# One stream of FFN blocks in written order: the scheduler is switched off for the main loop of a DFT + GeGLU kernel

## The chip, the cores and the metric

The kernel runs on one core of a Trainium2 chip. The metric is the device time of one execution in microseconds (us). Five engines work side by side, each on its own queue of instructions: TensorE (PE, with its weight loads shown as PEld), VectorE (DVE), ScalarE (ACT), GpSimd (POOL) and SyncE (SP). Transfers are issued from SP's queue, a few from ACT's, and the loads that change the type from POOL's.

## The reference

The input `x` has 8 batches of 3008 tokens with 256 channels. A two-dimensional Fourier transform over tokens and channels is taken of each batch and its real part kept; then every token goes through a gated feed-forward block (FFN) with 1536 hidden columns.

```
X = fft(fft(x, axis=1), axis=2).real          # x: (8, 3008, 256)
t = X.reshape(24064, 256)
out = (gelu(t @ w_gate) * (t @ w_val)) @ w_out # 256 -> 1536 -> 256
```

## The kernel before

**Half of the tokens carry all.** The transform of real input is symmetric, so for each batch only `HALF` = 1505 token columns are computed, split by symmetry into an even part E and an odd part O (`EO_sb`). E + O gives a token's value and E - O that of the mirrored token. The 1505 columns form three chunks of 512, 512 and 481.

**The transform of a batch** (`dft_work`) is a list of 37 entries, each a closure that issues a few instructions. Eight are `s1_pack`: eight small matmuls each of `x_sb` with `G` (`s1_mm`, L372) into two `ps_dft` banks, one copy by ACT to `up_sb` (L397) and two adds by DVE into `A_sb` (L400); each is followed by an empty entry. Twelve are `ch_pack` (four matmuls, L420, and a copy to `Z_sb`, L427). The remaining nine are `e_pack`, `b_pack` and `o_pack` for each chunk (L442, L470, L488), which write `EO_sb`, and `EB_sb` by a small trip through DRAM. Batch 0 is transformed in a head, which is written inside `tc.manual_schedule()`; the transform of batch b+1 is the *filler* in the FFN of batch b.

**The FFN of a batch** is 3 chunks x 12 hidden blocks = 36 blocks, called slots here. A block has five big matmuls (L541). Two, WgE and WgO, make the gate in `ps_g`, which ACT turns into `gelu_sb` (L557). WgM is then added to the same bank, which turns it into the mirrored gate, and ACT reads it again (L566). WvE makes the even value in `ps_v`; DVE reads it and adds channel 128, `ve_sb` (L575). WvO is added to the same bank; DVE multiplies gelu and value into `h_sb` (L586), makes the mirrored value `v_sb` (L588), and POOL multiplies that with the mirrored gelu into the second half of `h_sb` (L590). The second layer of a chunk is 24 pieces of four matmuls (L615) into `ps_o`; they run two per slot in the slots of the next chunk; each sixth piece is followed by a copy to `out_sb` on ACT (L635) and four stores on SP (L531).

**The order in which a slot is written** is that of the string `SLOT`:

```
SLOT = "GgVLvLf"   # G: gate, block fc   g: mirrored gate, block fc-1
                   # V: even value, fc   v: rest of the value, fc-1
                   # L: a second-layer piece   f: filler
```

Each chunk has a loop of 13 turns: the thirteenth does only `g` and `v` of the chunk's last block, and the next chunk starts with a turn that has no `g` and no `v`. The filler entries are spread evenly: entry count times (slot + 1) over 36.

**The input of the next transform.** `load_x` (L156) is one transfer for each half of a batch, issued on POOL's queue, which turns f32 into bf16 on the way, into one of two `x_sb` buffers. The call stands at the top of the batch loop: for b > 0, batch b+1 is loaded by the turn b of the loop, and `filler = dft_work(b + 1)` of the same turn reads it. The loads of batch 1 stand at the end of the head.

**What sets the order.** Inside `tc.manual_schedule()` each engine's queue has the instructions in the order in which the program writes them. Outside of it, as in the main loop before, Tile's scheduler puts them in order: it walks the same list with its own costs, and an instruction whose inputs are there may stand ahead of one that was written before it, on every engine, POOL's loads among them.

Of the kernel before, what the change touches and what calls it, by code (L numbers as in the profile page):

```python
# [18 lines left out]
def _sub(base: bass.AP, free_pattern, free_offset, part_start=0, part_num=None):  # L19
    p_step, p_count = base.ap[0]  # L20
    if part_num is None:
        part_num = p_count - part_start
    pat = [[p_step, part_num]] + [list(x) for x in free_pattern]
    off = base.offset + part_start * p_step + free_offset
    return ap_replace(base, ap=pat, offset=off)
# [11 lines left out]
def kernel(  # L37
# [10 lines left out]
    B, T, C = x.shape  # L48
# [6 lines left out]
    NFC = F // 128  # L55
# [3 lines left out]
    groups = [list(range(1, 9)), list(range(9, 17)), list(range(17, 24)) + [0]]  # L59
# [26 lines left out]
    G = const_pool.tile([NP, NJ, K2H * 4], BF16)  # L86
# [8 lines left out]
    def x_tile():  # L95
        return work_pool.tile([NP, NJ, C], BF16, tag="x", bufs=2, name="x_sb")
# [48 lines left out]
    x_tiles = []  # L145

    def x_src(b, p0, np_, j0, nj):
        return ap_replace(
            x,
            ap=[[NJ * C, np_], [1, nj * C]],  # L150
            offset=x.offset + (b * T + p0 * NJ + j0) * C,
        )

    def load_x(b, pieces):
        for j0, nj in pieces:
            nc.gpsimd.dma_start(out=_sub(x_tiles[b], [[1, nj * C]], j0 * C), in_=x_src(b, 0, NP, j0, nj))  # L156
# [176 lines left out]
    def fold_w(nm, q):  # L333
        def run():
            f0, n = WSL[q]
            fs = slice(f0, f0 + n)
            ps = ps_g() if nm == "g" else ps_v()
            nc.tensor.matmul(ps[:, :n], exch, w_hi[nm][:, fs], start=True, stop=True)  # L338
            lo = w_lo[nm][:, fs]
            nc.vector.scalar_tensor_tensor(W[nm, "E"][:, fs], ps[:, :n], keep, lo, op0=ALU.mult, op1=ALU.add)  # L340
            nc.vector.scalar_tensor_tensor(  # L341
                W[nm, "O"][:, fs], lo, keep, ps[:, :n], op0=ALU.mult, op1=ALU.subtract)
            if nm == "g":
                nc.scalar.activation(W[nm, "M"][:, fs], W[nm, "O"][:, fs], AF.Copy, scale=keep2)
        return run
# [308 lines left out]
    SLOT = "GgVLvLf"  # L654
# [52 lines left out]
    folds = {0: 1, 3: 2, 7: 3}  # L707
    folds = {slot: [fold_w(nm, q) for nm in ("g", "v")] for slot, q in folds.items()}
    early = head[NHEAD:]
    pend = []  # L710
    for b in range(B):
        if b + 1 < B:
            if b > 0:
                x_tiles.append(x_tile())
                load_x(b + 1, [(0, 16), (16, 16)])
            filler = dft_work(b + 1)
        else:
            filler = []
        chunks = ffn_work(b)
        nslot = len(chunks) * NFC  # L720
        first_slot = 0
        if b == 0:

            first_slot = NFC
        slot = 0
        fi = 0
        for parts, l2s in chunks:
            done = 0
            for fc in range(NFC + 1):
                for step in SLOT:  # L730
                    if step in "GV" and fc < NFC:
                        parts[step][fc]()
                    elif step in "gv" and fc > 0:
                        parts[step][fc - 1]()
                    elif step == "L" and done < len(pend) and fc < NFC:
                        pend[done]()
                        done += 1
                    elif step == "f" and fc < NFC:
                        if b == 0 and slot < NFC:
                            for _ in range(2):  # L740
                                if early:
                                    early.pop(0)()
                            for f in folds.get(slot, []):
                                f()
                        tgt = max(0, len(filler) * (slot + 1 - first_slot) // (nslot - first_slot))
                        while fi < tgt:
                            filler[fi]()
                            fi += 1
                slot += fc < NFC
            assert done == len(pend)  # L750
            pend = l2s
    for u in pend:
        u()

# [1 line left out]
_INS = ['x', 'moe_w_gate', 'moe_w_val', 'moe_w_out']  # L756
# [26 lines left out]
```

## Time and profile before

| | |
|---|---|
| three runs | 683.09 us median (682.94 to 683.29) |
| the profiled execution | 683.09 us, its span 681.3 us |
| PE busy | 643.4 us, 94% of the span |
| DVE busy | 631.2 us, 93% |
| ACT busy | 468.0 us, 69% |
| POOL busy | 356.0 us, 52% |
| first even value of batch 0 to that of batch 1 | 33.26 to 122.28 us |
| the same for batches 1 to 6 | 78.4 to 78.9 us each |
| batch 7, to its last `v_sb` | 593.81 to 664.15 us |
| `x_sb` loads, issue to landing | 6.6 to 16.0 us, median 9.1 us (14 loads) |

The span runs from the first to the last instruction; the 1.8 us between it and the profiled execution's own time lie outside the program's instructions. Busy is the time in which an engine had at least one instruction under way. Matmuls overlap in their pipeline, so that a PE that waits between two matmuls for less than the length of one still looks busy; the distance from one matmul's start to the next one's tells more. An instruction is named by engine, line and the tile that it writes: "PE ps_g L541" is a gate matmul.

### The profile page before, as it was taken

How to read it: one execution, taken by the hardware profiler on the slowest of the kernel's cores; microseconds unless marked ns; L12 is line 12 of the kernel's file. 1: busy time of each engine (PE TensorE's matmuls, PEld its weight loads, DVE VectorE, ACT ScalarE, POOL GpSimd, SP SyncE). 2: the span in 40 equal slices, each digit the busy share in tenths (PEclk: the TensorE clock that was granted, in tenths of full speed). 3: DMA queues.
4: the chain of work that ended last, by engine and by line, in shares of the span. 5: the costliest groups of instructions: out<-in, count | busy, mean ns of one | idle time of the engine just before them, and what ended most of it. 6: DMA issues, size and time to landing. Idle time of an engine off the chain costs nothing.

```text
span 681.3 us, 14441 instructions
## 1 busy us (share of the span) xinstructions
PE 643.4 (94%) x5038; PEld 432.2 (63%) x5092; DVE 631.2 (93%) x1067; ACT 468.0 (69%) x897; POOL 356.0 (52%) x345
## 2 busy tenths in 40 slices
PE   2787999999999999999999999999999999999995
PEld 1543656666666666676666666676666666666664
DVE  8699998999999999999899999999999999999990
ACT  4575668767777677776776777776777677766660
POOL 8334455456555555446554555445554545555650
PEclk9999999999999999999999999999999999999999
DMA  9780252216222342216212162221221112221123
GB/s 239 180 181 0 47 111 59 48 37 130 48 56 50 65 102 52 55 43 124 52 44 56 34 132 48 55 48 37 47 55 40 44 41 47 55 51 40 44 48 70
DMA packets 39684, 46.21 MB, mean 68 GB/s; under 512 B 7361, under 2 KB 36694, under 8 KB 38102
## 3 DMA queue, kind: packets, MB, share of 16 engines
q1 hardware_dynamic: 35834, 33.21, 20.3%
q0 software_dynamic: 3184, 11.57, 9.3%
q8 instruction: 40, 0.66, 0.4%
q10 hardware_dynamic: 592, 0.49, 0.3%
q14 instruction: 34, 0.28, 0.1%
HBM read 32.15 MB, written 24.66 MB: 83 GB/s over the span
## 4 chain that ended last, share of the span: by engine, by line
PE 82%; ACT 6%; DVE 4%; DMA 3%; issue 1%; SPq 0%; POOL 0%; ACTq 0%; DVEq 0%; POOLq 0%
PE ps_o L615 35%; PE ps_g L541 24%; PE ps_v L541 16%; DMA out_dram<-out_sb 3%; PE ps_dft L420 3%; PE ps_dft L372 2%; ACT gelu_sb L566 2%; DVE x_sb L243 2%; ACT gelu_sb L557 1%; ACT out_sb L635 1%; PE ps_dft L488 1%; PE ps_dft L442 1%; ACT Z_sb L427 1%; PE ps_g L338 1%; ACT EO_sb L492 1%
## 5 line engine op out<-in xcount | busy, mean ns | idle before, releaser
L590 POOL TENSOR_TENSOR h_sb<-gelu_sb,v_sb 128x512 bf16<-128x512 bf16 (+1 forms) x288 | 329.8, 1145 | 289.3 <-DVE v_sb L588 200.7
L615 PE MATMUL ps_o<-Wo_sb,h_sb 128*128 128x256 bf16 (+1 forms) x2232 | 341.8, 272 | 3.0 <-ACT gelu_sb L566 1.1
L615 PEld LDWEIGHTS <-h_sb 128*128 128x128 bf16 (+1 forms) x2304 | 228.6, 100 | 108.8 <-issue 3.3
L557 ACT ACTIVATE gelu_sb<-ps_g 128x512 bf16<-128x512 f32 (+1 forms) x288 | 169.6, 592 | 77.4 <-PE ps_g L541 59.7
L575 DVE SCALAR_TENSOR_TENSOR ve_sb<-EB_sb,w,ps_v 128x512 f32<-128x512 bf16 (+1 forms) x288 | 209.8, 731 | 9.4 <-PE ps_v L541 8.8
L586 DVE TENSOR_TENSOR h_sb<-gelu_sb,ps_v 128x512 bf16<-128x512 bf16 (+1 forms) x288 | 194.0, 674 | 12.0 <-ACT gelu_sb L557 5.2
L588 DVE SCALAR_TENSOR_TENSOR v_sb<-ve_sb,ps_v 128x512 f32<-128x512 f32 (+1 forms) x288 | 192.5, 668 | 0.0
L566 ACT ACTIVATE gelu_sb<-ps_g 128x512 bf16<-128x512 f32 (+1 forms) x288 | 169.5, 592 | 16.1 <-PE ps_g L541 15.7
L541 PE MATMUL ps_g<-EO_sb,WgE 128*128 128x512 bf16 (+1 forms) x285 | 107.0, 375 | 3.2 <-ACT gelu_sb L566 2.1
L541 PE MATMUL ps_v<-EO_sb,WvO 128*128 128x512 bf16 (+1 forms) x288 | 108.2, 376 | 0.6
L541 PE MATMUL ps_g<-EO_sb,WgM 128*128 128x512 bf16 (+1 forms) x282 | 104.7, 376 | 2.5 <-ACT gelu_sb L557 1.6
L541 PE MATMUL ps_v<-EO_sb,WvE 128*128 128x512 bf16 (+1 forms) x279 | 104.8, 376 | 0.1
L541 PE MATMUL ps_g<-EO_sb,WgO 128*128 128x512 bf16 (+1 forms) x252 | 94.7, 376 | 1.4 <-DVE WgO L341 1.3
L635 ACT ACTIVATE out_sb<-ps_o 128x512 f32<-128x512 f32 x92 | 55.0, 597 | 34.4 <-PE ps_o L615 28.5
L427 ACT ACTIVATE Z_sb<-ps_dft 128x512 bf16<-128x512 f32 x88 | 52.4, 599 | 16.2 <-PE ps_dft L420 15.9
L400 DVE TENSOR_TENSOR A_sb<-ps_dft,up_sb 128x384 bf16<-128x384 f32 x112 | 56.8, 548 | 4.8 <-ACT up_sb L397 4.8
L372 PEld LDWEIGHTS <-x_sb 94*128 94x128 bf16 x512 | 33.0, 101 | 29.1 <-DVE x_sb L243 19.1
L541 PEld LDWEIGHTS <-WvE 128*128 128x128 bf16 x288 | 28.1, 98 | 25.4 <-issue 3.3
L541 PEld LDWEIGHTS <-WgM 128*128 128x128 bf16 x288 | 28.1, 97 | 24.3
L397 ACT ACTIVATE up_sb<-ps_dft 128x384 f32<-128x384 f32 x56 | 27.5, 490 | 21.3 <-PE ps_dft L372 21.3
L420 PE MATMUL ps_dft<-CS,A_sb 128*128 128x128 bf16 x372 | 40.5, 222 | 1.2 <-ACT Z_sb L427 0.6
L372 PE MATMUL ps_dft<-G,x_sb 94*128 94x96 bf16 x468 | 35.6, 208 | 4.7 <-DVE x_sb L243 4.6
(104 smaller groups left out, 314.2 us busy)
## 6 DMA issues: line engine op xcount, KB each, us to landing
out_dram<-out_sb SPq DMA_DIRECT2D x361, 64.0 KB
x_sb<-in_x_dram POOLq DMA_DIRECT2D x14, 752.0 KB, 9.1
EB_sb<-row SPq DMA_DIRECT2D x14, 128.0 KB
x_plain<-in_x_dram SPq DMA_DIRECT2D x4, 384.0 KB
x_plain<-in_x_dram SPq DMA_DIRECT2D x2, 768.0 KB
EB_sb<-row SPq DMA_DIRECT2D x7, 120.2 KB
Wo_sb<-in_moe_w_out_dram POOLq DMA_DIRECT2D x2, 384.0 KB, 5.8
wg_hi<-in_moe_w_gate_dram SPq DMA_DIRECT2D x2, 256.0 KB
```

The lines of the kernel that those rows point to most:

```text
L372: nc.tensor.matmul(ps[:, jj * 96 : (jj + 1) * 96], xt[:, j0 + jj, cc * 128 : (cc + 1) * 128], G[:, j0 + jj, :], start=True, stop=True,)
L420: nc.tensor.matmul(ps[:, o : o + 128], A[:, g, k2 + d, :], CS[:, g, :], start=True, stop=True)
L427: nc.scalar.activation(dst, src, AF.Copy)
L541: nc.tensor.matmul(ps[:, :n], W[nm, part][:, fs], src, start=start, stop=stop, **kw)
L557: nc.scalar.activation(gl[:, 0, :n], pg[:, :n], AF.Gelu)
L566: nc.scalar.activation(_sub(gl, [[-1, n]], TOK + n - 1), pg[:, :n], AF.Gelu)
L575: nc.vector.scalar_tensor_tensor(ve[:, :n], EB_bufs[b][:, c0 : c0 + n], w128[:, fc : fc + 1], pv[:, :n], op0=ALU.mult, op1=ALU.add)
L586: nc.vector.tensor_tensor(st["h"][:, fc, 0, :n], gl[:, 0, :n], pv[:, :n], op=ALU.mult)
L588: nc.vector.scalar_tensor_tensor(_sub(vv, [[-1, n]], n - 1), ve[:, :n], 2.0, pv[:, :n], op0=ALU.mult, op1=ALU.subtract)
L590: nc.gpsimd.tensor_tensor(st["h"][:, fc, 1, :n], gl[:, 1, :n], vv[:, :n], op=ALU.mult)
L615: nc.tensor.matmul(pso[:m, sign, :], st["h"][:, fc, sign, h0 : h0 + m], Wo_sb[:, fc, :], start=(fc == 0), stop=(fc == NFC - 1),)
L635: nc.scalar.activation(osb[:m], pso[:m], AF.Copy)
```

## The change

The three nested loops become one function `feed` that is called inside `tc.manual_schedule()`. It lists all 288 blocks of all batches and walks them in one stream. A slot keeps its parts in the same order, gate, mirrored gate of the block before, even value, piece, rest of the value of the block before, piece, filler; the block before may now belong to the chunk or the batch before, so the turn with only `g` and `v` is left out except after the last block of all. The calls of `load_x` and `dft_work` are made at slot 0 of each batch, ahead of the slot's other parts. The pieces of the second layer, the early entries of batch 0, the weight folds and the spread of the filler are as before. The functions that issue the instructions are not changed, and neither are the pools.

```diff
@@ -707,50 +707,60 @@
     folds = {0: 1, 3: 2, 7: 3}
     folds = {slot: [fold_w(nm, q) for nm in ("g", "v")] for slot, q in folds.items()}
     early = head[NHEAD:]
-    pend = []
-    for b in range(B):
-        if b + 1 < B:
-            if b > 0:
-                x_tiles.append(x_tile())
-                load_x(b + 1, [(0, 16), (16, 16)])
-            filler = dft_work(b + 1)
-        else:
-            filler = []
-        chunks = ffn_work(b)
-        nslot = len(chunks) * NFC
-        first_slot = 0
-        if b == 0:
-
-            first_slot = NFC
-        slot = 0
-        fi = 0
-        for parts, l2s in chunks:
-            done = 0
-            for fc in range(NFC + 1):
-                for step in SLOT:
-                    if step in "GV" and fc < NFC:
-                        parts[step][fc]()
-                    elif step in "gv" and fc > 0:
-                        parts[step][fc - 1]()
-                    elif step == "L" and done < len(pend) and fc < NFC:
-                        pend[done]()
-                        done += 1
-                    elif step == "f" and fc < NFC:
-                        if b == 0 and slot < NFC:
-                            for _ in range(2):
-                                if early:
-                                    early.pop(0)()
-                            for f in folds.get(slot, []):
-                                f()
-                        tgt = max(0, len(filler) * (slot + 1 - first_slot) // (nslot - first_slot))
-                        while fi < tgt:
-                            filler[fi]()
-                            fi += 1
-                slot += fc < NFC
-            assert done == len(pend)
-            pend = l2s
-    for u in pend:
-        u()
+
+    def feed():
+        blocks, works = [], []
+        for b in range(B):
+            for parts, l2s in ffn_work(b):
+                works.append(l2s)
+                blocks += [(b, parts, fc) for fc in range(NFC)]
+        nslot = len(groups) * NFC
+        filler, fi = [], 0
+        pend, before = [], None
+        for i, (b, parts, fc) in enumerate(blocks):
+            slot = i % nslot
+            if slot == 0:
+                assert fi == len(filler)
+                if b + 1 < B:
+                    if b > 0:
+                        x_tiles.append(x_tile())
+                        load_x(b + 1, [(0, 16), (16, 16)])
+                    filler = dft_work(b + 1)
+                else:
+                    filler = []
+                fi = 0
+            if fc == 0 and i:
+                assert not pend
+                pend = list(works[i // NFC - 1])
+            parts["G"][fc]()
+            if before:
+                before[0]["g"][before[1]]()
+            parts["V"][fc]()
+            if pend:
+                pend.pop(0)()
+            if before:
+                before[0]["v"][before[1]]()
+            if pend:
+                pend.pop(0)()
+            before = parts, fc
+            if b == 0 and slot < NFC:
+                for _ in range(2):
+                    if early:
+                        early.pop(0)()
+                for f in folds.get(slot, []):
+                    f()
+            first_slot = NFC if b == 0 else 0
+            tgt = max(0, len(filler) * (slot + 1 - first_slot) // (nslot - first_slot))
+            while fi < tgt:
+                filler[fi]()
+                fi += 1
+        before[0]["g"][before[1]]()
+        before[0]["v"][before[1]]()
+        for u in works[-1]:
+            u()
+
+    with tc.manual_schedule():
+        feed()
 
 # ---- launch: one core; inputs and outputs as the reference has them ----
 _INS = ['x', 'moe_w_gate', 'moe_w_val', 'moe_w_out']
```

## Prediction

> **What bounds the kernel now.** I read the page first: busy shares, then the chain that ended last.
>
> ```profile
> PE 643.4 (94%) x5038; PEld 432.2 (63%) x5092; DVE 631.2 (93%) x1067; ACT 468.0 (69%) x897; POOL 356.0 (52%) x345
> PE 82%; ACT 6%; DVE 4%; DMA 3%; issue 1%; SPq 0%; POOL 0%; ACTq 0%; DVEq 0%; POOLq 0%
> ```
>
> Two engines are nearly full and the chain runs through PE. Next, the windows from the first even value of one batch to that of the next (columns: length; busy time of PE, PEld, DVE, ACT, POOL; clock; DMA).
>
> ```profile
> 200.89:279.46 78.57, 77.91 (x627) 53.14 (x633) 75.32 (x129) 56.90 (x110) 42.32 (x38) 1.00 0.30 65
> 593.81:664.15 70.34, 70.07 (x472) 46.91 (x476) 69.56 (x110) 43.86 (x83) 41.13 (x36) 1.00 0.21 47
> ```
>
> PE is busy for all but 0.7 us of a batch. Starts of matmuls in the timeline give its true price: 216 ns for 512 columns, 203.6 for 481, 109 for an L615, 43, 56 and 29 for the transform's. A block is 5 x 216 + 8 x 109 = 1952 ns (481 columns: 1890). A batch is 24 x 1.952 + 12 x 1.890 + fillers (8 x 0.344 + 12 x 0.224 + 6 x 0.23 + some 0.8 at b_pack) = 77.2 us, against 78.6: PE truly waits 1.4 us per batch. DVE's starts are 656, 597 and 598 ns apart in a block when nothing holds it (1.851 us), 0.93 us for the pair L400.
>
> **The step that matters** is the load of the next batch's `x_sb`. In the timeline (start, duration, engine, line), batch 2's turn of the loop issues the load of batch 3 on POOL long before batch 2 begins; the first load of this kind:
>
> ```profile
> 90.36 0.56 POOL L156 DMA_DIRECT2D x_sb<-in_x_dram  x1 [1.37 <-PE ps_g L541]
> ```
>
> It is read from 201.01 on. The next, issued at 154.21, is read here, at the start of batch 3:
>
> ```profile
> 278.28 1.11 POOL L590 TENSOR_TENSOR h_sb<-gelu_sb,v_sb 128x481 bf16<-128x481 bf16 x1 [1.01 <-DVE e_sb L474]
> 279.46 0.73 DVE L575 SCALAR_TENSOR_TENSOR ve_sb<-EB_sb,w,ps_v 128x512 f32<-128x512 bf16 x1
> 279.59 0.46 PEld L372 LDWEIGHTS <-x_sb 94*128 94x128 bf16 x8
> 279.69 0.51 PE L372 MATMUL ps_dft<-G,x_sb 94*128 94x96 bf16 x8
> 280.24 0.49 ACT L397 ACTIVATE up_sb<-ps_dft 128x384 f32<-128x384 f32 x1 [0.94 <-PE ps_dft L372]
> 280.76 1.02 DVE L400 TENSOR_TENSOR A_sb<-ps_dft,up_sb 128x384 bf16<-128x384 f32 x2 [0.57 <-ACT up_sb L397]
> ```
>
> The weight load L372 waits for nothing. What a load needs, for the pair issued at 311.4 and 313.1:
>
> ```profile
> L156 POOL DMA_DIRECT2D x_sb<-in_x_dram x2: 559/559/559, 311.4 to 313.1; - x2
> DMA to landing us min/median/max: 7.2/8.7/10.3
> ```
>
> The first half lands 7.2 us after its issue (7.3, 7.3 and 7.4 in the pairs at 232.8, 390.3 and 154.2; 6.6 at 90.4).
>
> [...] the scheduler placed every load of the main loop a batch ahead. [...] In the head, groups of four 128-column matmuls start 0.42 us apart, 106 ns each, where the main loop has 56:
>
> ```profile
> 24.91 0.63 PE L420 MATMUL ps_dft<-CS,A_sb 128*128 128x128 bf16 x4
> 25.33 0.63 PE L420 MATMUL ps_g<-CS,A_sb 128*128 128x128 bf16 x4
> 25.76 0.63 PE L420 MATMUL ps_v<-CS,A_sb 128*128 128x128 bf16 x4
> ```
>
> And after the last matmul, which ends at 673.6, the clock record falls to half at 678.1, 4.5 us later.
>
> **The change part by part.** I sum against the profiled execution, 683.09 us (span 681.3 and 1.8 around it), which is also the median of the runs.
>
> *1. The loads go back to where they are written.* In the changed order POOL's queue has, at each batch border, L590 of block 34, the two loads, L590 of block 35, and so on; PE's queue has the first eight L372 that read the first half at the end of the same slot 0. This holds at the starts of batches 1 to 6, six times; batch 0's filler reads loads that stay in the head, batch 7 has no filler. PE's work up to that L372 is the same set of matmuls as now, so it arrives at the time of now: 279.59. POOL is free at 278.28 + 1.11 = 279.39. The half lands at 279.39 + 7.3 = 286.7, so PE waits **7.1 us**. The other five borders give 7.1 too (POOL's end and L372 are 0.19 to 0.20 us apart in all). Behind the wait stand all later matmuls on PE; ACT's L397, DVE's L400 and everything after these wait in turn, as ACT and DVE keep written order too. DVE has only the rest of block 35 to do, 1.2 us. Nothing hides it: 6 x 7.1 = **+42.6 us**. The second half is read eight slots later and is hidden. The two issues, 1.12 us of POOL ahead of L590 of block 35, lie inside the wait: that product is first read two slots later. POOL's room, 48%, takes the rest. Bounds of the landing: 6.6 and the 9.7 us of the head's first load (29.2 to 38.9, beside the weights), since stores run beside it here: +38 to +57.
>
> *2. The clock.* 7 us of idle PE is over the 4.5 that halved it at the end. [...] the first matmuls cost double: L372 ends at +0.64 instead of +0.34, the next even value at +2.35 instead of +1.2, its rest at +3.6. Following the DVE queue through this (L400 0.3 late, L586 of block 36 at +3.8 instead of +2.8, L575 of slot 2 at +5.75 instead of +4.0), DVE is 2.0 us late when PE is fast again; PE's lost work is absorbed, since DVE sets the pace in the next slots. 6 x 2.0 = **+12 us**; bounds 0 (the clock holds) and 3 us each.
>
> *3. Written order inside a batch.* In slots 0 to 15, with L400 in each second, DVE needs 16 x 1.851 + 8 x 0.93 = 37.1 us and PE 34.0. From the first L400 to the end of slot 15 DVE already runs without a gap in the trace (slots 1 to 15 all at 1.85 or 2.78), and the written order does not shorten it. What differs is how far PE can get ahead meanwhile: in written order it stops at the rest of the value (L541 WvO) of block i until DVE has read `ve_sb` of block i, about one slot ahead. From the L372 of slot 0 DVE reaches the end of the 15th `ve_sb` at +35.3; from there PE has 0.88 (rest of slot 16) + 15.2 (to slot 23) + 25.8 (slots 24 to 35) + 1.9 (slot 0 up to L372) = 43.8 us. Sum 79.1 against 78.6 now: **+0.5 us** x 6 = +3. Bounds: -1.4 us (no wait of PE is left) and +1.5 (further stops behind ACT). A gain is not excluded.
>
> *4. Batch 0.* DVE sets the pace for 24 slots. Of its 64 us it idles 2.6 in several gaps, the largest 0.8 before an L400. Written order should close those before L400, but adds turns in which PE waits for `Z_sb` copies (e_pack in the early slots), and PE gets less far ahead for chunk 2. I take **-1.2**, between -2.6 and +3.
>
> *5. Borders and end.* A chunk's border turn without `g` or `v` has the same matmuls in other order: no PE gap stands there now, so 0. The stores keep SP's queue and count; the broadcast for `EB_sb` moves by one or two stores, and is needed 12 slots later: 0. After the last block both orders have the same 96 matmuls and stores: 0.
>
> Sum: 683.1 + 42.6 + 12 + 3 - 1.2 = 739.5, say **740 us**.
>
> **The rivals.**
> *The clock holds*: [...] Against: 4.5 us sufficed at the end. Then 683.1 + 42.6 + 3 - 1.2 = 727.5.
> *The landing is later*: four stores and an `EB_sb` broadcast are under way at the border, as at 29.2. At 9.7 us: 683.1 + 57 + 12 + 1.8 = 754.
> *In-order stops in each slot*: ACT's copies between the gelus hold `ps_g`, of which there are two. 0.1 us for 252 slots is +25: 765. Against: slots 24 to 35 stand in just this order now and run at PE's price.
> *Faster*: the load is hidden and PE's waits vanish: 6 x 1.4 + 2.6 = 11 us at best, 672. It decides if a border costs under 11 / 6 = 1.8 us, that is, if a half lands within 2.0 us of its issue; none did in under 6.6.
> That the loads are not where I place them is excluded by the order of the built program.
>
> **How the numbers follow.** Forecast 0.60, clock 0.16, late landing 0.14, in-order stops 0.08, faster 0.02. About 0.2% (1.4 us) is what a measurement here can tell from none. Faster 0.02, same 0.01, slower 0.97. The range, 722 to 758, takes in the clock case and the later landing and leaves out the stops and the gain; its lower end is the clock case with a landing of 6.6 us and the gains of steps 3 and 4 in part.
>
> **What would show it.** In the profile after: PEld L372 waiting for DMA x_sb six times, some 7 us each; L156 at the batch borders, first at some 121 us and then some 88 us apart; [...] slots 24 to 35 still at 2.0 to 2.1 us. I am wrong if L372 waits for nothing, or if the intervals between borders grow by far more than wait and clock.

## The result, and the profile after

The changed kernel takes 739.58 us (median; 738.97 to 740.28), the kernel before 683.02 us on the same chip: a ratio of 1.083, with a 95% interval of 1.081 to 1.085. The profiled execution took 738.97 us, its span is 737.2 us.

The first lines to read are again the busy shares and the chain of waits that ended last:

```profile
PE 652.3 (88%) x5036; PEld 436.4 (59%) x5092; DVE 640.4 (87%) x1067; ACT 467.6 (63%) x897; POOL 355.5 (48%) x345
...
PE 57%; DVE 24%; DMA 8%; issue 6%; ACT 3%; POOL 1%; ACTq 0%; SPq 0%; DVEq 0%; POOLq 0%
```

PE and DVE, 94% and 93% busy before, are at 88% and 87%. Each has 9 us more of busy time, in a span that is 55.9 us longer; so most of the added time is waiting. In the chain PE's share fell from 82 to 57%, and DMA, DVE and "issue" took it.

The windows from one batch's first even value to the next (start and end; then the columns of the prediction's windows: length; busy time of PE, PEld, DVE, ACT, POOL; clock; DMA) say where. The first row is batch 2, the second batch 7, which transforms nothing:

```profile
209.53:298.40 88.87, 79.51 (x627) 53.45 (x633) 76.83 (x128) 56.96 (x111) 42.22 (x39) 0.96 0.26 58
649.04:719.91 70.87, 70.55 (x476) 47.40 (x481) 70.13 (x111) 44.56 (x85) 41.13 (x36) 1.00 0.20 46
```

Batch 2 went from 78.57 to 88.87 us with nearly the same busy times, and its mean clock is 0.96. Batch 7 is 0.5 us longer. Batches 1 to 6, the six that read a load at their border to transform the next batch, sum to 526.64 us (649.04 less 122.40), against 471.53 before: +55.1 of the 55.9 us. Batch 0 ends 0.12 us later than before, batch 7 adds 0.5, the tail 0.1.

The waits of the whole kernel (what waited, for what: us in total, times, longest):

```profile
DVE A_sb L400 <- ACT up_sb L397: 37.0, 6, 7.8
PEld L372 <- DMA x_sb<-in_x_dram: 35.8, 6, 7.5
...
PE ps_dft L470 <- DVE e_sb L474: 6.6, 7, 0.9
```

Six waits for the load, 6.0 us each, that PE did not have before, and behind each of them one of DVE. The third line, a wait of PE for DVE inside `b_pack`, was not in the forecast. In the timeline of the border of batch 3 (start, duration, engine, line), POOL and then PE:

```profile
296.97 1.10 POOL L590 TENSOR_TENSOR h_sb<-gelu_sb,v_sb 128x481 bf16<-128x481 bf16 x1 [1.01 <-DVE e_sb L474]
298.01 1.06 POOL L156 DMA_DIRECT2D x_sb<-in_x_dram  x2
300.48 1.10 POOL L590 TENSOR_TENSOR h_sb<-gelu_sb,v_sb 128x481 bf16<-128x481 bf16 x1 [1.41 <-DVE v_sb L588]
```

```profile
295.87 0.20 PE L470 MATMUL ps_dft<-TPI,Z_sb 128*7 128x64 bf16 x1
297.00 0.18 PE L470 MATMUL ps_dft<-TPI,Z_sb 128*1 128x33 bf16 x1 [0.94 <-DVE e_sb L474]
...
298.84 0.60 PE L615 MATMUL ps_o<-Wo_sb,h_sb 128*128 128x256 bf16 x4
304.84 0.82 PE L372 MATMUL ps_dft<-G,x_sb 94*128 94x96 bf16 x8 [5.39 <-DMA x_sb<-in_x_dram]
305.46 0.63 PE L541 MATMUL ps_g<-EO_sb,WgE 128*128 128x512 bf16 x1
305.88 0.63 PE L541 MATMUL ps_g<-EO_sb,WgO 128*128 128x512 bf16 x1
```

The loads stand between the two L590, as the forecast placed them. The half issued at 298.01 lands 6.78 us later, at 304.8, and L372 starts with it. The gate matmuls that follow start 0.42 us apart where 0.216 is the full price. DVE over the same border, from its last work before the wait:

```profile
299.69 0.65 DVE L588 SCALAR_TENSOR_TENSOR v_sb<-ve_sb,ps_v 128x481 f32<-128x481 f32 x1
306.22 1.02 DVE L400 TENSOR_TENSOR A_sb<-ps_dft,up_sb 128x384 bf16<-128x384 f32 x2 [5.88 <-ACT up_sb L397]
...
308.68 0.69 DVE L586 TENSOR_TENSOR h_sb<-gelu_sb,ps_v 128x512 bf16<-128x512 bf16 x1 [0.53 <-PE ps_v L541]
...
310.59 0.75 DVE L575 SCALAR_TENSOR_TENSOR ve_sb<-EB_sb,w,ps_v 128x512 f32<-128x512 bf16 x1 [0.62 <-PE ps_v L541]
```

After 5.9 us of nothing DVE is held again by the cold PE (a PE at half clock), 0.5 and 0.6 us at a time. From slot 2 to slot 20 it then runs without a gap of 0.1 us, so it sets the pace there, and what the clock costs is this waiting of DVE rather than PE's slower matmuls as such; the run with PE kept busy, below, puts a number on it. The clock row of the page has 40 slices of 18.4 us. Four of the cold stretches show in it as eights, two are too short to show, and the last eight is the end of the kernel, when no matmul is left:

```profile
PEclk9999999999989999899998999999998999999998
```

The clock record has all six, at 128.84, 214.18, 302.92, 391.67, 480.41 and 565.75 us; those at 128.84 and 480.41 last 3.41 us, the other four 6.83.

### The profile page after: what moved, and what is told of

It is laid out like the page before. It is cut to its first block, busy times and chain, and to the rows that moved or that the text cites. A ratio compares the mean times of both kernels' runs of the same rounds, so it can differ in the third digit from the quotient of the medians.

```text
span 737.2 us, 14514 instructions
## 1 busy us (share of the span) xinstructions
PE 652.3 (88%) x5036; PEld 436.4 (59%) x5092; DVE 640.4 (87%) x1067; ACT 467.6 (63%) x897; POOL 355.5 (48%) x345
## 4 chain that ended last, share of the span: by engine, by line
PE 57%; DVE 24%; DMA 8%; issue 6%; ACT 3%; POOL 1%; ACTq 0%; SPq 0%; DVEq 0%; POOLq 0%
PE ps_o L615 23%; PE ps_g L541 17%; PE ps_v L541 11%; DVE ve_sb L575 7%; DVE h_sb L586 6%; DMA x_sb<-in_x_dram 6%; DVE A_sb L400 4%; DVE v_sb L588 4%; PE ps_dft L420 3%; DVE x_sb L243 1%; PE ps_dft L372 1%; DMA out_dram<-out_sb 1%; ACT gelu_sb L566 1%; POOL h_sb L590 1%; PE ps_dft L442 1%
## 5 line engine op out<-in xcount | busy, mean ns | idle before, releaser
L590 POOL TENSOR_TENSOR h_sb<-gelu_sb,v_sb 128x512 bf16<-128x512 bf16 (+1 forms) x288 | 329.7, 1145 | 355.2 <-DVE v_sb L588 291.9
L615 PE MATMUL ps_o<-Wo_sb,h_sb 128*128 128x256 bf16 (+1 forms) x2232 | 339.1, 275 | 1.0
L615 PEld LDWEIGHTS <-h_sb 128*128 128x128 bf16 (+1 forms) x2304 | 230.6, 101 | 124.3 <-issue 11.7
L575 DVE SCALAR_TENSOR_TENSOR ve_sb<-EB_sb,w,ps_v 128x512 f32<-128x512 bf16 (+1 forms) x288 | 211.1, 733 | 30.1 <-PE ps_v L541 20.4
L557 ACT ACTIVATE gelu_sb<-ps_g 128x512 bf16<-128x512 f32 (+1 forms) x288 | 170.1, 590 | 77.2 <-PE ps_g L541 71.1
L586 DVE TENSOR_TENSOR h_sb<-gelu_sb,ps_v 128x512 bf16<-128x512 bf16 (+1 forms) x288 | 194.2, 674 | 3.2 <-PE ps_v L541 2.3
L566 ACT ACTIVATE gelu_sb<-ps_g 128x512 bf16<-128x512 f32 (+1 forms) x288 | 170.2, 591 | 0.0
L541 PE MATMUL ps_g<-EO_sb,WgE 128*128 128x512 bf16 (+1 forms) x287 | 110.0, 383 | 4.9 <-ACT gelu_sb L566 2.9
L541 PE MATMUL ps_v<-EO_sb,WvO 128*128 128x512 bf16 (+1 forms) x288 | 109.0, 379 | 4.0 <-DVE ve_sb L575 4.0
L541 PE MATMUL ps_g<-EO_sb,WgM 128*128 128x512 bf16 (+1 forms) x286 | 109.0, 381 | 2.5
L541 PE MATMUL ps_v<-EO_sb,WvE 128*128 128x512 bf16 (+1 forms) x281 | 107.1, 381 | 0.1
L541 PE MATMUL ps_g<-EO_sb,WgO 128*128 128x512 bf16 (+1 forms) x242 | 92.8, 383 | 0.5 <-DVE WgO L341 0.5
L400 DVE TENSOR_TENSOR A_sb<-ps_dft,up_sb 128x384 bf16<-128x384 f32 x112 | 56.9, 548 | 37.6 <-ACT up_sb L397 37.0
L372 PE MATMUL ps_dft<-G,x_sb 94*128 94x96 bf16 x468 | 33.3, 216 | 40.6 <-DMA x_sb<-in_x_dram 34.1
L372 PEld LDWEIGHTS <-x_sb 94*128 94x128 bf16 x512 | 31.2, 105 | 58.2 <-DMA x_sb<-in_x_dram 35.8
L541 PEld LDWEIGHTS <-WvE 128*128 128x128 bf16 x288 | 28.4, 99 | 34.8 <-issue 2.0
L541 PEld LDWEIGHTS <-WgM 128*128 128x128 bf16 x288 | 28.5, 99 | 34.3 <-issue 2.5
L420 PE MATMUL ps_dft<-CS,A_sb 128*128 128x128 bf16 x372 | 35.9, 223 | 1.1 <-ACT EO_sb L492 1.1
```

The lines of the kernel that those rows point to most:

```text
L372: nc.tensor.matmul(ps[:, jj * 96 : (jj + 1) * 96], xt[:, j0 + jj, cc * 128 : (cc + 1) * 128], G[:, j0 + jj, :], start=True, stop=True,)
L400: nc.vector.tensor_tensor(dst, lo, up8, op=op)
L420: nc.tensor.matmul(ps[:, o : o + 128], A[:, g, k2 + d, :], CS[:, g, :], start=True, stop=True)
L541: nc.tensor.matmul(ps[:, :n], W[nm, part][:, fs], src, start=start, stop=stop, **kw)
L557: nc.scalar.activation(gl[:, 0, :n], pg[:, :n], AF.Gelu)
L566: nc.scalar.activation(_sub(gl, [[-1, n]], TOK + n - 1), pg[:, :n], AF.Gelu)
```

## The experiments

All times are medians; ratios are to the kernel before, run beside each on the same chip. Where an edit adds lines, the numbers behind it shift: in the runs of the last part, L545, L570 and L619 are the L541, L566 and L615 of the kernel before, L401 is its L400, and L403 is the copy that replaces the second add.

### Early loads, all else in written order

```diff
-                    if b > 0:
-                        x_tiles.append(x_tile())
-                        load_x(b + 1, [(0, 16), (16, 16)])
...
+            if slot == 17 and b + 2 < B:
+                x_tiles.append(x_tile())
+                load_x(b + 2, [(0, 16), (16, 16)])
```

> The changed kernel with one thing moved: the loads of x_sb for batch b+2 are called at slot 17 of batch b, some 40 us before slot 0 of batch b+1 reads them; all else stays in written order. Theory (late loads and the cold clock after them are the loss, written order itself costs about 1 us per batch): 689 us, 686 to 692; no wait of L372 for x_sb, clock 1.00 throughout the main loop, borders 79.5 us apart. Rival (written order stalls the engines and the wait for x_sb only covers these stalls): above 715 us. Rival (written order by itself is faster than the scheduler's, since DVE no longer idles before L400): below 682 us.

693.14 us (692.89 to 693.99), ratio 1.016 (1.014 to 1.017). L372 waits for no DMA, the mean clock is 0.997, and borders come 80.16 us apart (80.71 once). So late loads and what they bring cost 739.58 - 693.14 = 46.4 us, and written order by itself about 10 us, 1.6 per batch. This is more than the 0.5 of the forecast, and the time is above the range that was expected of this run. One line of the waits is left at the border:

```profile
PE ps_dft L470 <- DVE e_sb L474: 6.5, 7, 0.9
```

### The same loads two slots ahead of the border

```diff
-            if slot == 17 and b + 2 < B:
+            if slot == 34 and b + 2 < B:
```

> The same loads called at slot 34, two slots (4.2 us) before the border instead of at it. Theory: PE waits 6.0 - 4.2 = some 1.7 us at each of six borders, too short to halve the clock, so 689 + 6 x 1.7 = 699 us (693 to 704) with clock 1.00. Rival (the cost comes with each load at the border, from its traffic beside the stores, whatever the lead): 725 us or more. Rival (every wait of PE costs the clock too): 710 us with a clock under 1.00.

699.45 us (699.31 to 699.62), ratio 1.025 (1.023 to 1.026). L372 waits 1.2 us at each of six borders (7.4 in total), and the clock does not fall (0.998 on the mean). Against the early loads this is 6.3 us, 1.05 per border: a wait of about 1 us, after which the clock stayed full, costs about what it shows, and no more.

### The same late load, with PE kept busy

Ahead of the first L372 of each border PE runs 26 matmuls of 512 columns into a bank that nobody reads.

```diff
+            if slot == 0 and 0 < b < B - 1:
+                ps = ps_dft()
+                for _ in range(26):
+                    nc.tensor.matmul(
+                        ps[:, :512], W["g", "E"][:, 0:128], EO_bufs[b][:, 0, 0:512], start=True, stop=True)
```

> The changed kernel with 26 more matmuls of 512 columns (26 x 0.216 = 5.6 us) on PE just ahead of the first L372 of each border, into a ps_dft bank that nobody reads: PE works through the wait for x_sb instead of standing still; the loads stay where they are. Theory (cold clock costs some 1.7 us per border): 739.6 - 6 x 1.7 = 729.5 us (726 to 733), clock 1.00 in the main loop, the wait of L372 down from 6.0 to under 1 us. Rival (the clock costs nothing, DVE and ACT set the restart): 739 to 741 us. Rival (the matmuls add to the path): 745 us or more.

727.63 us (727.16 to 728.26), ratio 1.066 (1.064 to 1.068). The clock is full from 32.8 us to the last matmuls, and five of the borders come 85.81 us apart, one 86.65. PE does more work than in the changed kernel and the whole is 739.58 - 727.63 = 11.95 us faster: the clock costs 2.0 us per border. The border of batch 3, PE and then DVE (L757 are the extra matmuls):

```profile
294.59 5.77 PE L757 MATMUL ps_dft<-EO_sb,WgE 128*128 128x512 bf16 x26
300.20 0.55 PE L372 MATMUL ps_dft<-G,x_sb 94*128 94x96 bf16 x8
304.10 0.74 DVE L575 SCALAR_TENSOR_TENSOR ve_sb<-EB_sb,w,ps_v 128x512 f32<-128x512 bf16 x1
```

DVE starts the even value of slot 2 (L575) 3.90 us after the L372. In the changed kernel it is 5.75 us (310.59 against 304.84), 0.62 of it a wait for PE that this run does not have: in this way PE's half clock reaches the time. At three borders L372 shows no wait for the load at all, so there the extra matmuls may have ended after it landed; if so, the clock's price is a little more.

### The old loops inside the written order

The three nested loops of the kernel before, indented under `with tc.manual_schedule():`, nothing else.

> The nested loops of the kernel before, unchanged, but inside manual_schedule: written order without the one stream. Theory: nearly all of the loss is there too; and since the border turn now has g and v of block 35 ahead of the loads, POOL issues them after L590 of block 35 instead of block 34, some 1.4 us later, at six borders: 739.6 + 8 = 748 us (743 to 752). Rival (the stream itself is the loss): 683 to 695 us. Rival (the order at the border is of no weight): 738 to 741 us.

758.08 us (757.9 to 758.8), ratio 1.111 (1.109 to 1.113), above the range that was expected. The timeline of DVE and POOL at the border of batch 3 shows why:

```profile
304.03 0.74 DVE L575 SCALAR_TENSOR_TENSOR ve_sb<-EB_sb,w,ps_v 128x512 f32<-128x512 bf16 x1
304.25 1.10 POOL L590 TENSOR_TENSOR h_sb<-gelu_sb,v_sb 128x481 bf16<-128x481 bf16 x1 [1.32 <-DVE v_sb L588]
305.30 1.06 POOL L156 DMA_DIRECT2D x_sb<-in_x_dram  x2
```

In the old loops the thirteenth turn writes the last block's L590 before the next batch begins, so the loads stand behind it on POOL: 1.27 us after the batch's first even value, where the changed kernel issues them 0.39 us before it (298.01 against 298.40). PE, whose order also lacks `g` and `v` there, reaches L372 sooner. Its six waits sum to 51.4 us, 8.6 each, and at four borders the clock stays at half for 10.24 us. The stream itself is thus worth 758.08 - 739.58 = 18.5 us when both are in written order; 15.6 of them are in these waits (51.4 against 35.8), and the rest was not separated.

### The stream in the scheduler's order

```diff
-    with tc.manual_schedule():
-        feed()
+    feed()
```

> The changed kernel's one stream of blocks, but without manual_schedule around it: the scheduler orders the main loop again. Theory (the loss came with the written order of the loads, not with the stream): 683 us, 680 to 686, loads of x_sb a batch ahead as in the kernel before. Rival (dropping the border turn with g and v alone costs or gains by itself): below 678 or above 690 us.

680.28 us (678.39 to 680.99), ratio 0.995 (0.993 to 0.997): by its median the fastest kernel of those that compute everything. The scheduler walks the new list and takes the loads a batch ahead, as it did before; the view of the loads' line shows the last issued at 389.8 us, while batch 7's transform begins at 513, and it lists nobody who waited for it:

```profile
L156 POOL DMA_DIRECT2D x_sb<-in_x_dram x14: 538/559/589, 28.9 to 389.8; - x14
```

So the loss belongs to the written order and not to the stream. Batch 0 is shorter (87.68 us against 89.03), so are batches 1 to 6 (470.25 against 471.53 in sum), and batch 7 gives 0.7 back; which of the moved parts brings the gain was not separated.

### What written order costs beyond the loads

Starting from the early loads, `b_pack` issues all its matmuls (L470) ahead of its copies (L474):

```diff
                 for i, (off, k2, nk, w) in enumerate(runs):
                     nc.tensor.matmul(
                         ps[:nk, i * K1 : i * K1 + w], _sub(st["Z"], [[C, nk]], k2 * C + 128), TPI[:, 0:w],
                         start=True, stop=True)
+                for i, (off, k2, nk, w) in enumerate(runs):
                     e128 = e128_tile()
```

> As the run with loads at slot 17 (693.1 us), and in b_pack of batches 1 to 7 both matmuls L470 are written ahead of both DVE copies L474, so that the second matmul no longer waits for the first copy. Theory (the 0.94 us wait of PE for e_sb in slot 35, seven times, is on the path, since PE sets the pace there): 693.1 - 7 x 0.94 = 686.5 us (685 to 688.5). Rival (PE is ahead there and the wait is free): 692 to 694 us.

686.2 us (685.01 to 686.63), ratio 1.004 (1.003 to 1.005), a border each 79.06 us (79.77 and 79.23 for the first two). The 0.94 us wait is gone and a border is 1.1 us shorter. It had come from the copy that stands between two matmuls into one bank: they write different columns, and the second still waited 0.94 us for DVE's copy of the first.

Next, on top of it, `s1_pack` every third slot instead of every second, so that DVE's load is thinner in the early slots:

```diff
+            if b > 0 and filler:
+                if slot < 23:
+                    tgt = 2 * (slot // 3 + 1)
+                else:
+                    tgt = 16 + -(-(slot - 22) * 21 // 13)
```

> As the run before (early loads, L470 ahead of L474), and in batches 1 to 6 the eight s1_pack entries are put three slots apart (slots 0 to 21) instead of two (0 to 14), the other 21 entries in slots 23 to 35. Theory (what written order still loses is PE waiting for DVE in the slots with L400, because PE gets only about one slot ahead): DVE needs 23 x 1.851 + 8 x 0.93 = 50.0 us for slots 0 to 22 and PE 47.7, a difference of 2.4 instead of 3.1 in 16 slots, most of it covered by PE's lead; borders 78.0 us apart instead of 79.2: 679 us (677 to 684), faster than the kernel before. Rival (ACT's copies of the crowded fillers in slots 23 to 35 hold PE): 686 us or more.

683.57 us (682.28 to 684.25), ratio 1.001 (1.000 to 1.002). Borders come 78.72 us apart, not 78.0: it gains a third of what was expected there. With both pieces (L) ahead of the rest of the value on top of that:

```diff
-            if pend:
-                pend.pop(0)()
+            for _ in range(2):
+                if pend:
+                    pend.pop(0)()
             if before:
                 before[0]["v"][before[1]]()
-            if pend:
-                pend.pop(0)()
```

> As the run with s1_pack every third slot (683.6 us), and both second-layer pieces of a slot stand ahead of WvO of the block before instead of one on each side, so that PE does 0.44 us more before it has to wait for ve_sb. Theory (PE's lead over DVE limits it in the slots with L400; DVE starts L586 later too, so of the 0.44 only about half is gained): 0.2 to 0.4 us per batch, 682 us (680.5 to 683). Rival (DVE gets WvO later than it needs it): 684 us or more.

681.23 us (680.3 to 682.79), ratio 0.998 (0.997 to 0.999): written order can be brought below the kernel before by 0.2%. Borders are 78.36 us apart; batch 0 gave 1.1 us of that back (89.99 us against 88.89). The same kernel with the scheduler's order:

> Kernel: all edits of e9_spread_late_v (early loads, b_pack's matmuls first, s1_pack over every third slot, both pieces ahead of the rest of the value), but feed() runs without manual_schedule, so the scheduler orders the queues. Theory A (the scheduler gains by moving what written order fixes, and the spread takes DVE's load off the early slots as well): a border every 77.6 to 78.0 us instead of 78.27 in e5_stream_scheduled, so 676 to 679 us. Theory B (the scheduler already spread what could be spread): as e5_stream_scheduled, 680 us within 1. Theory C (the scheduler's walk undoes the spread and puts the copies badly): 682 us or more.

685.32 us (683.54 to 686.01), ratio 1.003 (1.002 to 1.004). A list spread for written order is worse for the scheduler than the plain one (borders 78.7 to 79.2 us).

### Is it DVE that holds PE?

Three kernels take half of L400 away from DVE, each on top of early loads with `b_pack` reordered. In all three the differences of the transform are not formed. First the second add became a copy on ACT of `lo`:

```diff
-                    nc.vector.tensor_tensor(dst, lo, up8, op=op)
+                    if g == 0:
+                        nc.vector.tensor_tensor(dst, lo, up8, op=op)
+                    else:
+                        nc.scalar.activation(dst, lo, AF.Copy)
```

> As the run with early loads and L470 ahead of L474 (686.2 us, borders 79.06 us apart), but in s1_pack of batches 1 to 7 the second of the two DVE adds L400 is left out and ACT copies the bank instead, so that part of the transform is not computed; it only takes load off DVE. Theory (what written order still loses is PE waiting for DVE in slots 0 to 19): DVE then needs 16 x 1.851 + 8 x 0.47 = 33.4 us for slots 0 to 15 against PE's 34.0, PE sets the pace in all slots, borders 77.2 to 77.5 us apart: 686.2 - 6 x 1.7 = 676 us (674 to 679). Rival (ACT's one more copy holds PE, or the rest is PE's own issue time): 684 us or more.

721.22 us (720.91 to 721.65), ratio 1.056 (1.054 to 1.059): 35 us slower, where 10 us less was expected. The waits:

```profile
PE ps_g L545 <- ACT gelu_sb L570: 43.6, 60, 1.0
ACT A_sb L403 <- DVE A_sb L401: 35.4, 56, 0.9
```

ACT's copy reads the bank that DVE's first add is reading, and waits for it 0.63 us, 56 times. Behind it on ACT's queue stand the gelus, and behind those PE's next gate. So this run measured that wait, and says nothing on DVE. With the copy reading `hi`, which ACT itself has just read:

```diff
-                        nc.scalar.activation(dst, lo, AF.Copy)
+                        nc.scalar.activation(dst, hi, AF.Copy)
```

> Kernel: early loads and b_pack's matmuls ahead of its copies (e6_early_b), and in s1_pack the second add of DVE (L400) is replaced by a copy on ACT of the bank that ACT itself has just read (hi), so this copy waits for nothing of DVE's. Part of the transform is left out: the differences are not formed. Theory (what written order still costs in e6_early_b is DVE in slots 0 to 19): DVE has 8 x 0.46 = 3.7 us less per batch, PE sets the pace in all slots, a border comes every 77.3 to 77.6 us instead of 79.06, so 686.2 - 6 x 1.6 = 676 us (674 to 679). Rival (any further work on ACT between two gelus holds the gates, whether it waits or not): the 8 copies of some 0.5 us each per batch go onto PE, 6 x 4 = 24 us less what DVE gives, so 690 us or more. Second rival (PE is held by something else): 684 to 687 us.

681.23 us (680.13 to 682.07), ratio 0.997 (0.996 to 0.998), between what the theory and the second rival expected. The copy no longer waits: at 287.71 us it starts ahead of DVE's add, at 287.84, and runs beside it, though both write `A_sb`; so the wait of the run before was for the bank. Batch 0 is 1.9 us shorter, but a border still takes 78.77 us. In the timeline of batch 3, PE's and ACT's lines:

```profile
288.55 0.62 ACT L570 ACTIVATE gelu_sb<-ps_g 128x512 bf16<-128x512 f32 x1
288.64 0.60 PE L619 MATMUL ps_o<-Wo_sb,h_sb 128*128 128x256 bf16 x4
...
289.22 0.38 PE L545 MATMUL ps_g<-EO_sb,WgE 128*128 128x512 bf16 x1
```

The four L619 are done in 4 x 109 ns, at 289.08; the gate starts at 289.22, just after the second gelu, at 289.17, has left its bank. PE is held by ACT for 0.14 us here; that the copy had pushed the gelus back is the likely reason. None of the three expectations was met, and the run does not decide. So the copy went to POOL, which reads `up_sb`:

```diff
-                        nc.scalar.activation(dst, hi, AF.Copy)
+                        nc.gpsimd.tensor_copy(dst, up8)
```

> Kernel: early loads and b_pack's matmuls ahead of its copies (e6_early_b), and DVE's second add of each s1_pack is replaced by a copy of up_sb on POOL, which has room and stands in no gate's way. Part of the transform is left out: the differences are not formed. Both e6_early_b and this have the same work on PE and ACT; only DVE loses 8 x 0.46 = 3.7 us per batch. In e11_half_add_hi the same relief brought a border every 78.77 us instead of 79.06, but with the copy on ACT between two gelus, and PE's starts showed gaps of 0.14 to 0.30 us at WgE behind the second gelu. Theory (the rest of written order's price is DVE's load in slots 0 to 19): a border every 77.2 to 77.8 us and batch 0 2 us shorter, 686.2 - 6 x 1.5 - 2 = 675 us (673 to 678). Rival (PE is held by ACT or by itself, DVE's load is not what counts): a border every 78.6 to 79.0 us as with the copy on ACT, 681 us or more.

672.32 us (671.38 to 672.96), ratio 0.985 (0.983 to 0.988). The windows of batch 3, with DVE's full load (early loads and `b_pack` reordered) and with the lighter one:

```profile
280.42:359.48 79.06, 78.10 (x634) 52.86 (x633) 76.33 (x129) 56.85 (x111) 42.23 (x39) 1.00 0.29 65
```

```profile
272.52:349.70 77.18, 76.80 (x627) 52.97 (x633) 73.59 (x120) 56.85 (x111) 45.82 (x47) 1.00 0.30 67
```

ACT's busy time is the same to 0.01 us, DVE's is 2.7 us less, and the batch is 1.9 us shorter. 77.18 is the price that the prediction had summed for PE from its matmul starts (77.2): PE then waits for next to nothing. One rival lies near: without DVE's second add the transform's bank comes free sooner. It can be left aside, since in batches 1 to 6 of the kernel with DVE's full load no L372 waits for that bank. So DVE's load in the early slots is what holds PE in written order once the loads are early and `b_pack` is reordered. It is not a price of written order alone: the kernel before, at 78.6 us a batch, also stands 1.4 above PE's price, and the scheduler's order was not run with the lighter load. Nor was a kernel that still forms the differences, but not on DVE.

## Why the prediction was right, point by point

The sum was 739.5, and 739.58 was measured. The mechanism is the one that was told, late loads and the half clock behind them. That the sum came out to 0.1 us is in part luck, since its parts did not all hold.

**Step 1, the loads.** The place, the number and the landing were right: six loads between the two L590 of blocks 34 and 35, landing 7.07 us after issue on the mean (6.52 to 8.65; 7.3 was taken). The wait was sized 7.1 us and is 6.0 by the trace; by the runs it is (739.58 - 693.14 - 11.95) / 6 = 5.7. The term that failed is "PE's work up to that L372 is the same set of matmuls as now, so it arrives at the time of now": the set is the same, but in written order PE is held 0.94 us at the second L470 of slot 35, and so comes later to a load whose landing does not depend on it. That all later matmuls of PE stand behind the wait, as the forecast took for granted, this trace shows: in the 5.39 us at batch 3's border no matmul passes the waiting L372, though the gate behind it, at 305.46, reads the `EO_sb` that slot 0's gate had read at 297.35. One reading of the trace before was off, with no effect on the sum: the load at 90.36 was not the first that the scheduler had moved ahead; batch 2's, at 30.27 and 41.37, was.

**Step 2, the clock.** 12 us forecast, 11.95 by the run with PE kept busy; by the windows of the two profiled executions it is 526.64 - 515.71 = 10.9, so the close agreement is partly luck. The mechanism is as told, DVE late by 2 us behind a cold PE: L586 of block 36 was forecast at +3.8 us after the load and L575 of slot 2 at +5.75, and in the changed kernel they start at +3.84 and +5.75. The rival in which the clock holds, 727.5, is close to what that run took (727.63). Half clock lasts 6.83 us at four borders and 3.41 at two, 5.7 on the mean. No trace from before the change shows how long PE stays at half clock after a pause, so the 2.0 us per border rest on an assumption of the author's.

**Step 3, order inside a batch.** The step summed 79.1 us per batch. Written order without late loads gave 80.16, and 79.06 once `b_pack` was reordered: the total of the step's reckoning, DVE's pace to slot 15 and PE's after it, was right to 0.1 us. That is in part luck, since in that run DVE runs without a gap to slot 20 and not only to 15. (Its reading that slots 1 to 15 of the kernel before are all at 1.85 or 2.78 us is nearly so: three of them are at 3.05, 1.59 and 1.87, the same in sum to 0.02.) That DVE's load is the cause is shown by the run with POOL's copy. What the step did not contain is the wait at L470.

**Step 5, the borders.** This is the step that failed: "no PE gap stands there now, so 0". There is none in the scheduler's order, because that order fills the time between the two L470 with other matmuls. In the timeline of the kernel before, at the border of batch 3, both and what stands between them:

```profile
277.18 0.20 PE L470 MATMUL ps_dft<-TPI,Z_sb 128*7 128x64 bf16 x1
277.31 0.39 PE L488 MATMUL ps_dft<-TPI,Z_sb 128*128 128x64 bf16 x8
277.55 0.36 PE L541 MATMUL ps_g<-EO_sb,WgM 128*128 128x481 bf16 x1
277.75 0.37 PE L541 MATMUL ps_v<-EO_sb,WvO 128*128 128x481 bf16 x1
277.96 0.38 PE L541 MATMUL ps_g<-EO_sb,WgE 128*128 128x512 bf16 x1
278.17 0.38 PE L541 MATMUL ps_g<-EO_sb,WgO 128*128 128x512 bf16 x1
278.48 0.18 PE L470 MATMUL ps_dft<-TPI,Z_sb 128*1 128x33 bf16 x1
```

The twelve matmuls between them (eight L488, four L541) are written behind the second L470 and stand ahead of it here. In written order the time between is a gap of 0.94 us, which the early-load kernels price at 693.14 - 686.2 = 6.9 us. In the changed kernel six of the seven gaps lie ahead of the longer wait for the load and shorten it, so they should cost next to nothing there; this is read from the trace, and no run has the late loads without the gap. The wait was oversized by about as much as the gap is long. So the two errors, steps 1 and 5, take each other up.

**Step 4, batch 0.** -1.2 forecast, +0.1 measured: it starts 1.55 us earlier (31.71 against 33.26) and has lost this by its end. This was not followed further.

**The rivals.** A later landing, 9.7 us, did not occur (8.65 at most). In-order stops in every slot would be 25 us; written order with early loads costs 10 in all, 6.9 of it in one gap per batch. A gain needed borders that cost under 1.8 us each; they cost 9.2.

## What to carry to other kernels

When a loop goes from the scheduler to written order, list first what the scheduler had moved ahead, the loads above all: each goes back to the line where it is written, and its price is landing time less the work that is left for the waiting engine, once per turn. Here such a wait cost more than it showed where the clock fell (PE standing for 5.1 us and more: 6.0 us of wait and a price of 46.4 / 6 = 7.7 per border), and just itself where the clock stayed full (1.2 us of wait, a price of 1.05). In these written orders an instruction that waited for another engine's read of the same bank held what was queued behind it (PE's second L470 for 0.94 us, ACT's copy for 0.63), so a matmul, copy, matmul sequence like this one wants its matmuls first, and work that is moved to a "free" engine must not stand between what the bottleneck waits for.

## What the runs showed of the hardware that was not expected

The half-clock stretches of the changed kernel last 3.41 or 6.83 us, at four borders of the old loops 10.24 (mean clock 0.961 there, 0.974 in the changed kernel), so much the same wait is paid differently from border to border. The six borders of the changed kernel, from PE's line and the clock record (us):

| border of batch | PE's last matmul ends | L372 starts | pause | clock falls | after the last matmul | at half clock |
|---|---|---|---|---|---|---|
| 1 | 123.44 | 128.83 | 5.40 | 128.84 | 5.41 | 3.41 |
| 2 | 210.57 | 217.83 | 7.26 | 214.18 | 3.61 | 6.83 |
| 3 | 299.44 | 304.84 | 5.39 | 302.92 | 3.48 | 6.83 |
| 4 | 387.31 | 392.99 | 5.68 | 391.67 | 4.36 | 6.83 |
| 5 | 475.75 | 480.98 | 5.24 | 480.41 | 4.67 | 3.41 |
| 6 | 562.43 | 567.57 | 5.14 | 565.75 | 3.31 | 6.83 |

The length does not follow the pause: 5.40 us at batch 1 led to 3.41 us of half clock, 5.39 at batch 3 to 6.83, and 7.26 at batch 2 to no more than 5.14 at batch 6. The two short stretches are those in which the clock fell latest, 5.41 and 4.67 us after the last matmul, against 3.31 to 4.36 at the other four. Pauses of 7.7 to 8.7 us in the old loops led to 6.83 or 10.24 us. What sets the moment of a fall and the length of a stretch was not shown.

And a wait of 0.63 us on ACT, 56 times, made a kernel with less work on DVE 35 us slower than the one with early loads and `b_pack` reordered: PE's waits for the second gelu, which stand behind it, came to 43.6 us.
